# The shift of the weight decode as an integer product on GpSimd, and values scaled by two products

## The chip, the cores and the metric

The kernel runs on one core of a Trainium2 chip. The metric is the device time of one execution in microseconds. In the words of the profile, PE is TensorE's matmuls and PEld its weight loads, DVE is VectorE, ACT is ScalarE, POOL is GpSimd and SP is the engine that issues most DMAs.

## The reference

Attention with normalised queries and keys, and a feed-forward layer behind it. Inputs q and k are single precision, the four weight matrices come in double precision (the kernel sees each as pairs of 32-bit words).

```python
q_n, k_n = rmsnorm(q, g_q), rmsnorm(k, g_k)          # (8, 12, 448, 64)
attn = softmax(q_n @ k_n.T / sqrt(64)); attn_out = attn @ v
x = attn_out as (8 * 448, 768)
h = max(x @ w1, x @ w2, x @ w3)                      # each 768 x 768
out = h @ w_out                                      # (3584, 768)
```

## The kernel before

**The work.** There are 8 batches of 12 heads. Two heads of one batch are a group (48 groups). A group's keys and queries are squared, their squares summed, and rows scaled by the inverse root (a power, L387); the scores of a group are made in four parts of 112 rows for both heads. Each part goes from TensorE (L545 or L553) to VectorE's row maximum (L562), to ScalarE's exponentials (L570, L579), and after a transposition to TensorE again, which multiplies with the values (L692 or L703). The first six groups (`PLAIN`) use single precision in all matmuls. From group 6 on every operand is split into two half-precision parts: ScalarE makes the upper part, GpSimd or VectorE the lower (L440 for keys and queries, L531 for values, L665 for attention weights), and values are first scaled on GpSimd by a factor of the batch (`scale_v`, L517). When six groups of a batch are done, its feed-forward layer enters a queue from which TensorE gets some matmuls in each beat (L732, L796).

**The order.** It is written out by hand: the program runs rounds of twelve beats, one round a group, and each engine executes its instructions strictly in the order in which the beats issue them. `later(n, work, True)` puts work at the end of the beat n beats ahead. In round g (beats 0 to 11), GpSimd gets the squares of group g + 2 at beats 0 (keys) and 3 (queries); VectorE sums them at beats 2 and 5 (L372); GpSimd makes the inverse roots at beats 5 and 7 (L383, L387) and scales keys at beat 8 (L419, L423) and queries at beat 9 (L394, and L406 for groups from 6 on). VectorE makes row maxima at beats 2, 5, 8 and 11.

**The weight blocks.** The weights come as 24 blocks of 128 x 768 doubles: 18 of w1, w2, w3, then 6 of w_out. The doubles become floats by integer steps. ScalarE multiplies the upper words, read as floats, by a power of two (`rebias`, L188), which moves their exponent. Then `decode` makes the bits of the float in three stages, one beat after another: stage 0 (L196) shifts the upper word left by three, stage 1 (L200) puts back its sign bit, stage 2 (L205) puts in three bits of the lower word. All three are on VectorE before. Stages 1 and 2 read two tiles, the raw words and the float. A block starts at beats 1, 5 and 9 of rounds 0 to 5, and every eight beats after that, until the sixth block of w_out in round 9. Its three stages are issued 2, 3 and 4 beats later, at the ends of those beats: stage 0 at beats 3, 7, 11, and stage 1 at beats 4, 8, and 0 of the next round. When three blocks are there, VectorE takes their largest value (L170, 2304 columns), and later ScalarE scales them and makes the upper part (L268, L269), and GpSimd the lower part (L272).

Of the kernel before, what the change touches and what calls it, by code (L numbers as in the profile page):

```python
# [10 lines left out]
U32 = mybir.dt.uint32  # L11
F16 = mybir.dt.float16
AF = mybir.ActivationFunctionType
ALU = mybir.AluOpType
AX = mybir.AxisListType.X

P = 128
# [22 lines left out]
def qknorm_attention_maxout_ffn_kernel(  # L40
# [35 lines left out]
    nc = tc.nc  # L76
    B, H, S, D = q.shape
    DM, DF = w1.shape
    DO = w_out.shape[1]
    NP = H // 2  # L80
# [12 lines left out]
    const = ctx.enter_context(tc.tile_pool(name="const", bufs=1))  # L93
# [40 lines left out]
    half_neg = const.tile([P, 15], F32, name="half_neg")  # L134
    nc.vector.memset(half_neg, -0.5)

    sums = [const.tile([P, 15], F32, name=f"ss{i}") for i in range(2)]
    for t in sums:
        nc.vector.memset(t, 1.0)
# [50 lines left out]
    def decode(raw, f, stage):  # L190

        bits = raw.rearrange("p (n t) -> p n t", t=2)
        upper, lower = bits[:, :, 1], bits[:, :, 0]
        f = f.bitcast(U32)
        if stage == 0:
            nc.vector.tensor_scalar(  # L196
                out=f, in0=upper, scalar1=3, scalar2=None, op0=ALU.logical_shift_left
            )
        elif stage == 1:
            nc.vector.scalar_tensor_tensor(  # L200
                out=f, in0=upper, scalar=0x80000000, in1=f,
                op0=ALU.bitwise_and, op1=ALU.bitwise_or,
            )
        else:
            nc.vector.scalar_tensor_tensor(  # L205
                out=f, in0=lower, scalar=29, in1=f,
                op0=ALU.logical_shift_right, op1=ALU.bitwise_or,
            )
# [25 lines left out]
    def prep_block(n):  # L234
        kind, ft, j = blocks[n]
        raw = raws[n]
        f = plain(w_sb, n) if kind == "in" else plain(wo_sb, ft)
        rebias(raw)

        for stage in range(3):  # L240
            later(2 + stage, lambda stage=stage: decode(raw, f, stage), True)
        if kind == "out":
            later(5, lambda: row_largest(o_row[:, ft:ft + 1], f), True)
        later(5, load_raw)
        if j == NJ - 1:
            later(5, lambda: bound_in(ft), True)
        elif kind == "out" and ft == NFT - 1:
            later(6, bound_out)
# [234 lines left out]
    v_up = const.tile([P, B], F32, name="v_up")  # L483
# [31 lines left out]
    def scale_v(g):  # L515
        vr = st[g]["vr"]
        nc.gpsimd.tensor_scalar(  # L517
            out=vr, in0=vr, scalar1=v_up[:, g // NP:g // NP + 1], scalar2=None,
            op0=ALU.mult,
        )  # L520

    def upper_v(g):
# [338 lines left out]
    for i, src in enumerate((g_q, g_k)):  # L861
        nc.scalar.dma_start(
            out=gains[:, i], in_=src.rearrange("(o d) -> o d", o=1).broadcast_to([P, D])
# [61 lines left out]
    def beat(g, i):  # L925
# [80 lines left out]
        if PLAIN <= g < G and i == 9:  # L1006
            scale_v(g)
# [61 lines left out]
```

## Time and profile before

| what | value |
|---|---|
| runs, us | 1098.79, 1097.26, 1098.78; median 1098.78 |
| span of the profiled execution, us | 1101.6 |
| granted TensorE clock, mean | 0.957 |
| busy, us: PE / DVE / ACT / POOL | 1018.6 / 757.8 / 772.1 / 702.4 |
| the 24 shifts (L196) on VectorE, us | 11.8 (18 of w1 to w3) and 6.7 (6 of w_out) |
| the 42 value scalings (L517) on GpSimd, us | 60.7 |

The profiled execution has no device time of its own beside its span, which lies 2.8 us above the median of the runs. A row of a group says how many instructions it has, their busy time and mean, and how long the engine sat idle just before them and for whom. A row in order of time begins with its start and its length in microseconds. In the rows of stretches each engine has its busy time and the number of its instructions. Rounds can be told apart by the rows of `finish` (L718), one a round at its tenth or eleventh beat: in rounds 2 to 6 they start at 77.93, 99.83, 120.56, 142.66 and 168.33 us.

### The profile page before, as it was taken

What the parts mean: (1) busy time and instruction counts of PE and PEld (TensorE: products, weight loads), DVE (VectorE), ACT (ScalarE), POOL (GpSimd) and SP (SyncE); (2) the same over time, 40 slices, a digit from 0 to 9 for tenths busy, and PEclk for the clock granted to TensorE, in tenths of its full rate; (3) what the DMA queues carried; (4) which work ended last, traced back from release to release, by engine and by line L of the source; (5) the groups of instructions that cost most, each with busy time, mean ns of one, the idle gap of its engine ahead of it and who ended that gap; (6) DMA issues with size and microseconds to landing.
All of it is one profiled execution on the core that took longest, in us unless ns stands there. A gap on an engine that the chain in (4) does not pass through costs nothing. (4 is left out here: it accounts for less than half of the span.)

```text
span 1101.6 us, 18390 instructions
## 1 busy us (share of the span) xinstructions
PE 1018.6 (92%) x6168; PEld 501.9 (46%) x6168; DVE 757.8 (69%) x1390; ACT 772.1 (70%) x1767; POOL 702.4 (64%) x805
## 2 busy tenths in 40 slices
PE   4678768988999999999999999999999999999998
PEld 2334333434444455444544454444444454445555
DVE  3899988888667676677677776777677766762210
ACT  4599887767868678687877777778777787773001
POOL 5477988856767767678677686776867677610000
PEclk9687868998989999999999999999999999999999
DMA  5554466856787679877888789787877798563002
GB/s 149 165 164 152 129 180 137 179 115 125 151 166 149 134 151 172 160 148 133 176 155 149 136 169 175 141 151 150 170 146 143 145 166 153 106 106 73 1 1 58
DMA packets 426654, 152.29 MB, mean 138 GB/s; under 512 B 372928, under 2 KB 422336, under 8 KB 426560
## 3 DMA queue, kind: packets, MB, share of 16 engines
q1 hardware_dynamic: 425888, 150.75, 66.8%
q8 instruction: 48, 0.79, 0.3%
q10 hardware_dynamic: 672, 0.38, 0.1%
q14 instruction: 46, 0.38, 0.1%
HBM read 51.97 MB, written 11.01 MB: 57 GB/s over the span
## 5 line engine op out<-in xcount | busy, mean ns | idle before, releaser
L732 PE MATMUL acc<-xt,w_sb 128*128 128x448 f16 x2592 | 520.6, 356 | 0.6 <-ACT m L742 0.6
L732 PEld LDWEIGHTS <-w_sb 128*128 128x128 f16 x2592 | 245.1, 99 | 262.9 <-issue 53.1
L562 DVE TENSOR_REDUCE sc<-sc 112x2 f32<-112x896 f32 x192 | 209.7, 1092 | 47.8 <-PE sc L553 46.6
L579 ACT ACTIVATE sc<-sc,nm,down 112x448 f32<-112x448 f32 x336 | 234.2, 697 | 11.2
L655 ACT ACTIVATE pp<-sc,rs 112x448 f16<-112x448 f32 x336 | 194.8, 632 | 48.5 <-ACT sc L579 40.4
L665 DVE SCALAR_TENSOR_TENSOR pp<-sc,rs,pp 112x448 f16<-112x448 f32 x336 | 212.9, 675 | 3.4 <-ACT pp L655 2.9
L387 POOL TENSOR_TENSOR ri<-ri,half_neg 128x7 f32<-128x7 f32 x96 | 154.2, 1606 | 8.0
L553 PE MATMUL sc<-kt,qt 64*112 64x448 f16 x1008 | 133.7, 371 | 27.1 <-DVE pp L665 23.6
L570 ACT ACTIVATE nm<-sc,down 112x2 f32<-112x2 f32 x192 | 50.7, 264 | 149.5 <-DVE sc L562 148.2
L796 PE MATMUL acc<-wo_sb,ht 128*128 128x384 f16 x864 | 151.4, 330 | 1.4 <-DVE ht L756 0.8
L761 POOL COPY hx<-ht 128x128 f16<-128x128 f16 x48 | 15.5, 323 | 197.7 <-DVE ht L756 191.7
L796 PEld LDWEIGHTS <-ht 128*128 128x128 f16 x864 | 82.0, 99 | 67.5 <-issue 14.5
L703 PE MATMUL av<-pt,vp 128*64 128x448 f16 x1008 | 108.3, 356 | 0.0
L553 PEld LDWEIGHTS <-qt 64*112 64x112 f16 x1008 | 55.0, 128 | 96.9 <-issue 56.4
L648 DVE TENSOR_SCALAR rs<-sc 112x2 f32<-112x2 f32 x168 | 26.6, 158 | 94.7 <-ACT sc L579 94.7
L440 POOL TENSOR_TENSOR kp<-kn,kp 128x512 f16<-128x512 f32 x42 | 50.0, 1190 | 58.9 <-ACT kp L434 58.9
L703 PEld LDWEIGHTS <-vp 128*64 128x64 f16 x1008 | 49.6, 108 | 56.0 <-issue 30.4
L718 DVE SCALAR_TENSOR_TENSOR xt<-av,xt 128x448 f16<-128x448 f32 x42 | 26.2, 625 | 71.1 <-ACT xt L717 71.1
L372 DVE TENSOR_REDUCE ss<-sq 128x7 f32<-128x448 f32 x96 | 60.9, 635 | 10.6 <-ACT sq L363 6.6
L531 POOL TENSOR_TENSOR vp<-vr,vp 128x448 f16<-128x448 f32 x42 | 43.8, 1044 | 32.2 <-ACT vp L525 32.1
L440 POOL TENSOR_TENSOR qp<-qn,qp 112x512 f16<-112x512 f32 x42 | 49.3, 1173 | 21.0 <-ACT qp L434 20.8
L517 POOL TENSOR_SCALAR vr<-vr,v_up 128x448 f32<-128x448 f32 x42 | 60.7, 1446 | 0.0
(112 smaller groups left out, 1203.1 us busy)
## 6 DMA issues: line engine op xcount, KB each, us to landing
raw<-in_moe_w_dram SPq DMA_DIRECT2D x18, 768.0 KB, 4.4
qr<-in_q_dram SPq DMA_DIRECT2D x48, 224.0 KB, 3.0
vr<-in_v_dram SPq DMA_DIRECT2D x96, 96.0 KB, 2.5
kr<-in_k_dram SPq DMA_DIRECT2D x95, 96.0 KB, 3.0
raw<-in_moe_w_out_dram SPq DMA_DIRECT2D x6, 768.0 KB, 5.1
pt<-pp SPq DMA_TRANSPOSE x168, 4.1
out_dram<-osb SPq DMA_DIRECT2D x8, 336.0 KB, 3.2
out_dram<-osb SPq DMA_DIRECT2D x8, 288.0 KB, 3.7
```

Of the source, the lines that this page charges most:

```text
L372: nc.vector.tensor_reduce(sums[g % 2][:sq.shape[0], KQ[what]], sq, axis=AX, op=ALU.add)
L387: nc.gpsimd.tensor_tensor(out=ri, in0=ri, in1=half_neg[:, at], op=ALU.pow)
L440: nc.gpsimd.tensor_tensor(out=parts[:, 1], in0=n, in1=parts[:, 0], op=ALU.subtract)
L517: nc.gpsimd.tensor_scalar(out=vr, in0=vr, scalar1=v_up[:, g // NP:g // NP + 1], scalar2=None, op0=ALU.mult,)
L553: nc.tensor.matmul(sc[:QP, h, :S], qt[rows, qp, c], kt[rows, kp, KEYS[h]], start=n == 0, stop=n == len(TERMS) - 1,)
L562: nc.vector.tensor_reduce(sc[:QP, 0, S + 8:S + 10], sc[:QP, :, :S], axis=AX, op=ALU.max, negate=True)
L579: nc.scalar.activation(to, sc[:QP, h, :S], AF.Exp, bias=nm[:, h:h + 1], scale=down[:QP], accum_out=total,)
L655: nc.scalar.activation(pp[:, 0, h], sc[:QP, h, :S], AF.Copy, scale=rs[:, h:h + 1])
L665: nc.vector.scalar_tensor_tensor(out=pp[:, 1, h], in0=sc[:QP, h, :S], scalar=rs[:, h:h + 1], in1=pp[:, 0, h], op0=ALU.mult, op1=ALU.subtract,)
L703: nc.tensor.matmul(av[half, :S], vp[rows, group, vpart], pt[rows, 7 * wp + group], start=u == 0 and n == 0, stop=u == 3 and n == len(TERMS ...
L732: nc.tensor.matmul(acc[:, :S], wt[:, wp, c], xs[c][:, xp], start=(c == 0 and n == 0), stop=(c == NCT - 1 and n == 2),)
L796: nc.tensor.matmul(acc[:, :HW], lhs, wo_sb[:, f, wp, half * HW:(half + 1) * HW], start=(f == 0 and n == 0), stop=(f == NFT - 1 and n == 2),)
```

## The change

Stage 0 is issued on GpSimd: the upper word times eight, both unsigned integers, where the eight is one column that is broadcast over the 768. Its place in the program, the end of its beat, is the same. A constant column is set once at the start. The value scaling on GpSimd gets a second product with 1.0 in the same instruction.

```diff
+    eight = const.tile([P, 1], U32, name="eight")
+    nc.vector.memset(eight, 8)
...
         if stage == 0:
-            nc.vector.tensor_scalar(
-                out=f, in0=upper, scalar1=3, scalar2=None, op0=ALU.logical_shift_left
+            nc.gpsimd.tensor_tensor(
+                out=f, in0=upper, in1=eight.broadcast_to([P, DM]), op=ALU.mult
             )
...
         nc.gpsimd.tensor_scalar(
-            out=vr, in0=vr, scalar1=v_up[:, g // NP:g // NP + 1], scalar2=None,
-            op0=ALU.mult,
+            out=vr, in0=vr, scalar1=v_up[:, g // NP:g // NP + 1], scalar2=1.0,
+            op0=ALU.mult, op1=ALU.mult,
         )
```

Every line of the kernel behind the constant stands three lines further down after the change (L196 becomes L199, L200 becomes L203, L372 becomes L375).

GpSimd's rows from the second inverse root (beat 7) of round 4 to the squares at beat 0 of round 5, before. `ri` are the inverse roots, `kn` the scaled keys, `qn` the queries, `w_sb` the weights; the number behind a name tells two buffers apart:

```order
L383 TENSOR_SCALAR ri<-ss_86 128x8
L387 TENSOR_TENSOR ri<-ri,half_neg 128x8
L419 TENSOR_TENSOR kn_90<-kr,ri 128x3x64
L423 TENSOR_TENSOR kn_90<-kr,ri 64x64
L419 TENSOR_TENSOR kn_90<-kr,ri 128x3x64
L423 TENSOR_TENSOR kn_90<-kr,ri 64x64
L272 TENSOR_TENSOR w_sb<-w_sb 128x768
L394 TENSOR_TENSOR qn<-qr,ri 112x2x4x64
L406 TENSOR_TENSOR qn<-qn,gain 112x512
L365 TENSOR_TENSOR sq<-kr 128x448
```

The same stretch of GpSimd after the change:

```order
L386 TENSOR_SCALAR ri<-ss_88 128x8
L390 TENSOR_TENSOR ri<-ri,half_neg 128x8
L199 TENSOR_TENSOR w_sb<-raw,eight 128x768
L422 TENSOR_TENSOR kn_92<-kr,ri 128x3x64
L426 TENSOR_TENSOR kn_92<-kr,ri 64x64
L422 TENSOR_TENSOR kn_92<-kr,ri 128x3x64
L426 TENSOR_TENSOR kn_92<-kr,ri 64x64
L275 TENSOR_TENSOR w_sb<-w_sb 128x768
L397 TENSOR_TENSOR qn<-qr,ri 112x2x4x64
L409 TENSOR_TENSOR qn<-qn,gain 112x512
L199 TENSOR_TENSOR w_sb<-raw,eight 128x768
L368 TENSOR_TENSOR sq<-kr 128x448
```

Two products (L199) have come into it: one between the inverse root and the keys, one between the queries and the next squares. The third product of a round stands behind the squares of the queries at beat 3.

VectorE's rows from the end of `finish` in round 3 to the row maximum at beat 2 of round 4, before (`xt` is the attention's result, `sc` the scores, `w_most` and `w_up` the scale of three blocks):

```order
L718 SCALAR_TENSOR_TENSOR xt<-av,v_up,xt 128x448
L562 TENSOR_REDUCE sc<-sc 112x2
L196 TENSOR_SCALAR w_sb<-raw 128x768
L259 TENSOR_SCALAR w_most<-most 128x1
L262 RECIPROCAL w_up<-w_most 128x1
L263 TENSOR_SCALAR w_up<-w_up 128x1
L200 SCALAR_TENSOR_TENSOR w_sb<-raw,w_sb 128x768
L205 SCALAR_TENSOR_TENSOR w_sb<-raw,w_sb 128x768
L562 TENSOR_REDUCE sc<-sc 112x2
```

The same stretch of VectorE after:

```order
L721 SCALAR_TENSOR_TENSOR xt<-av,v_up,xt 128x448
L565 TENSOR_REDUCE sc<-sc 112x2
L262 TENSOR_SCALAR w_most<-most 128x1
L265 RECIPROCAL w_up<-w_most 128x1
L266 TENSOR_SCALAR w_up<-w_up 128x1
L203 SCALAR_TENSOR_TENSOR w_sb<-raw,w_sb 128x768
L208 SCALAR_TENSOR_TENSOR w_sb<-raw,w_sb 128x768
L565 TENSOR_REDUCE sc<-sc 112x2
```

The shift is gone from it, and L203 reads what GpSimd's product wrote.

## The prediction

> **What bounds the kernel now.** I read the page first, then the busy time by stretches, then the groups of instructions of the two engines that the change touches, and last their rows in order of time in the rounds that mattered.
>
> ```profile
> span 1101.6 us, 18390 instructions
> core 0: us, PE busy (x) PEld busy (x) DVE busy (x) ACT busy (x) POOL busy (x), PEclk, DMA share, GB/s
> 20.00:60.00 40.00, 27.43 (x139) 14.93 (x140) 30.63 (x42) 24.92 (x61) 21.42 (x26) 0.74 0.48 143
> 80.00:150.00 70.00, 52.47 (x269) 26.96 (x269) 65.21 (x81) 63.08 (x138) 61.37 (x49) 0.74 0.50 147
> 150.00:245.00 95.00, 80.53 (x446) 36.48 (x442) 83.07 (x139) 69.72 (x150) 73.30 (x72) 0.89 0.72 153
> 245.00:1000.00 755.00, 739.36 (x4655) 359.94 (x4656) 540.37 (x1062) 574.46 (x1340) 522.24 (x622) 0.99 0.77 148
> ```
>
> From 245 us on TensorE is busy 739.36 of 755 us: it is the bound, and whatever is late or early by then is carried to the end undiminished. All weight blocks are decoded before that. In 80 to 150 us the bound is VectorE, 65.21 of 70 us, with GpSimd close behind at 61.37; in 150 to 245 us nothing is full. So the change is decided in the first 245 us. That VectorE is waited for there shows in the chain of waits of 10 to 245 us, where ScalarE's softmax stands behind VectorE's row maximum, and TensorE's scores behind that softmax (total, times, longest):
>
> ```profile
> ACT nm L570 <- DVE sc L562: 27.4, 12, 5.0
> PE sc L545 <- ACT e L579: 14.8, 12, 4.0
> ```
>
> The shift that goes, the step after it, and the nearest relative of the product that comes (minimum/median/maximum ns); then the shift's sums, for 80 to 150 us and for w_out's blocks; last the value scaling:
>
> ```profile
> L196 DVE TENSOR_SCALAR w_sb<-raw x18: 537/550/1326, 23.2 to 144.3; 128x768 uint32<-128x768 uint32 x18
> L205 DVE SCALAR_TENSOR_TENSOR w_sb<-raw,w_sb x18: 936/954/4292, 29.4 to 148.3; 128x768 uint32<-128x768 uint32 x18
> L272 POOL TENSOR_TENSOR w_sb<-w_sb x18: 1630/1640/1907, 66.8 to 200.2; 128x768 f16<-128x768 f32 x18
> L196 DVE TENSOR_SCALAR w_sb<-raw 128x768 uint32<-128x768 uint32 x10 | 5.9, 591 | 0.0
> L196 DVE TENSOR_SCALAR wo_sb<-raw 128x768 uint32<-128x768 uint32 x6 | 6.7, 1110 | 0.1
> L517 POOL TENSOR_SCALAR vr<-vr,v_up x42: 1400/1410/2230, 169.1 to 982.2; 128x448 f32<-128x448 f32 x42
> ```
>
> L205 has a median of 954 ns and a maximum of 4292. That worst one, with GpSimd's rows beside it:
>
> ```profile
> 123.80 1.65 POOL L365 TENSOR_TENSOR sq<-kr 128x448 f32<-128x448 f32 x1
> 124.69 4.29 DVE L205 SCALAR_TENSOR_TENSOR w_sb<-raw,w_sb 128x768 uint32<-128x768 uint32 x1
> 125.41 1.64 POOL L272 TENSOR_TENSOR w_sb<-w_sb 128x768 f16<-128x768 f32 x1
> 127.00 1.16 POOL L440 TENSOR_TENSOR kp<-kn,kp 128x512 f16<-128x512 f32 x1
> 128.12 1.87 POOL L440 TENSOR_TENSOR qp<-qn,qp 112x512 f16<-112x512 f32 x1
> ```
>
> It ended at 128.98; 0.95 us before that is 128.03, just before GpSimd went from one row to the next. So VectorE's steps with two inputs stand still while GpSimd works on large tiles, and GpSimd's do the same in turn: the same shape at L440 took 1.16 without VectorE, and the next, smaller one 1.87. The Trainium skill (SBUF — State Buffer, "Who interferes with whom") says that a VectorE instruction with two SBUF inputs contends with a GpSimd instruction that reads SBUF, under a lock that the first one holds whole. The rows of this case agree for large tiles.
>
> **The change, term by term.** I write M for one product on GpSimd. No row shows an integer product. The floor is the same width as a subtraction, 1.64 us (L272); the other end is the slowest elementwise rate of the rows, L517, 1.41 x 768 / 448 = 2.42 us. I take the middle, 2.0 us, since integers are further from both. Below nothing is excluded: it is an added instruction on its engine.
>
> *VectorE's side*: 24 shifts go. At 0.55 us undisturbed that is 13.2 us; a shift, too, was at times blocked (1.11 us on average for w_out).
>
> *The rounds before 78 us* (9 blocks): 9 x 0.55 = 5.0 us of VectorE at most. But in 20 to 60 us VectorE is idle for 9.4 of 40 us, on loads, ScalarE and TensorE, and GpSimd for 18.6, so M finds room and the shift had room too. One thing costs: in the first round M of the third block stands ahead of the next squares on GpSimd and waits for ScalarE's rebias of it.
>
> ```profile
> 33.55 0.93 POOL L365 TENSOR_TENSOR sq<-kr 128x448 f32<-128x448 f32 x1
> 40.72 0.88 ACT L188 ACTIVATE raw<-raw 128x768 f32<-128x768 f32 x1 [2.96 <-DMA raw<-in_moe_w_dram]
> ```
>
> The squares that ran at 33.55 now start after 41.6 + M = 43.6. I take -0.5, ends -5 and +3.
>
> *Rounds 3, 4 and 5 (78 to 143 us)*, the term that decides. In each round two of the three M stand where GpSimd's work after the second sum of squares (L372) leads to VectorE's first decode step of the next round (L200): one ahead of the keys, one after the queries. Before, these ends of GpSimd's stretch held up nobody. Now L200 must wait for them. Each round's L200, its reduction L372 of q, the shift between them, and the end of GpSimd's stretch:
>
> ```profile
> 80.45 1.34 DVE L200 SCALAR_TENSOR_TENSOR w_sb<-raw,w_sb 128x768 uint32<-128x768 uint32 x1
> 88.98 0.55 DVE L196 TENSOR_SCALAR w_sb<-raw 128x768 uint32<-128x768 uint32 x1
> 91.44 0.68 DVE L372 TENSOR_REDUCE ss<-sq 112x8 f32<-112x512 f32 x1
> 98.98 1.76 POOL L394 TENSOR_TENSOR qn<-qr,ri 112x512 f32<-112x512 f32 x1
> 102.35 1.23 DVE L200 SCALAR_TENSOR_TENSOR w_sb<-raw,w_sb 128x768 uint32<-128x768 uint32 x1
> 109.88 0.99 DVE L196 TENSOR_SCALAR w_sb<-raw 128x768 uint32<-128x768 uint32 x1
> 112.78 0.68 DVE L372 TENSOR_REDUCE ss<-sq 112x8 f32<-112x512 f32 x1
> 122.22 1.61 POOL L406 TENSOR_TENSOR qn<-qn,gain 112x512 f32<-112x512 f32 x1
> 123.08 1.57 DVE L200 SCALAR_TENSOR_TENSOR w_sb<-raw,w_sb 128x768 uint32<-128x768 uint32 x1
> 132.96 0.55 DVE L196 TENSOR_SCALAR w_sb<-raw 128x768 uint32<-128x768 uint32 x1
> 135.41 0.68 DVE L372 TENSOR_REDUCE ss<-sq 112x8 f32<-112x512 f32 x1
> 145.79 1.85 POOL L406 TENSOR_TENSOR qn<-qn,gain 112x512 f32<-112x512 f32 x1
> 145.18 1.35 DVE L200 SCALAR_TENSOR_TENSOR w_sb<-raw,w_sb 128x768 uint32<-128x768 uint32 x1
> ```
>
> Round 3: from L200 to the end of L372, 92.12 - 80.45 = 11.67, less its shift 0.55; from there to the end of GpSimd's stretch, 100.74 - 92.12 = 8.62; with 2 M = 4.0 the way round is 23.74 us, against 102.35 - 80.45 = 21.90 now: +1.8. Round 4: 11.11 - 0.99 + 10.37 + 4.0 = 24.49 against 20.73: +3.8. Round 5: 13.01 - 0.55 + 11.55 + 4.0 = 28.01 against 22.10: +5.9. Together +11.5. That counts twice what the two engines make each other wait: while VectorE stands still behind M it blocks nobody, and a single L205 here holds 3.3 us of such waiting (4.29 - 0.95). I take 1.5 us a round off, 4.5 in all: **+7**. M counts six times in it: with 1.64 it is +4.8, with 2.42 +9.5. Behind L200 in VectorE's queue stand L205 and then the row maximum L562, for which ScalarE and TensorE wait as above, so this is paid in full. The third M of a round, ahead of the conversion of the weights at L272, has the room in which GpSimd now waits and costs nothing; without that room it would cost up to M each, 6 us.
>
> *Rounds 6 to 9 (143 to 245 us)*: six blocks, one every eight beats. Six shifts worth 6.7 us go from VectorE, which is behind here: TensorE waits for it before its scores.
>
> ```profile
> PE sc L553 <- DVE pp L665: 13.0, 7, 3.9
> ```
>
> GpSimd is busy 73.3 of 95 us and takes 6 M = 12 more, without a loop as above since only one M lies on the way and the rounds are longer. But keys and queries come up to M later. I take -2; ends -6.7 and +6.
>
> *Values (L517)*: 42 instructions, none before 169.1 us. A second product could make one as short as the squares of this width, 0.93 us (L365 at 33.55), or add the part that goes by elements again, up to twice 1.41. Where TensorE is busy 98% of the time this costs and gains nothing; its cover would have to be worn through by 42 x 1.41 = 59 us on GpSimd, which has 755 - 522 = 233 us idle there. Only four or so lie before 245 us: 0, ends -2 and +6. The memset of the constant (one column, once) is nothing.
>
> Sum: -0.5 + 7 - 2 + 0 = **+4.5 us**. The profiled execution has a span of 1101.6 us, 2.8 above the median of the runs, 1098.78; I take the profile's difference onto the median: 1103.3 us. About 0.2%, 2.2 us, is what a measurement of this kernel can tell from no change.
>
> **The rivals.** *Relief of VectorE*: VectorE is the fullest engine in 80 to 150 us and loses 10 shifts, 5.9 us, and half of w_out's 6.7; GpSimd, no longer blocked by shifts, has M done before L200 asks. For it: the shift's maximum of 1326 ns and w_out's mean of 1110 show that shift and GpSimd blocked each other. Against it: the three rounds above, where GpSimd's end lay at most 1.6 us before L200 (100.74 against 102.35) and after it in the other two. It decides where two M fit into what the mutual waiting gives back: M under about 0.8 us by my term for these rounds (7 - 6 x 1.2 = 0). Part of the 9.3 us will be lost to other engines; I price it at -7: 1091.8 us.
>
> *A slow integer product*: the power at L387 shows that an operation can cost GpSimd far more than a product of floats. At M = 3.2 the three rounds get 6 x 1.2 = 7 more, the two rounds before them close the same way (+2 each), and four later rounds lose about 1 each: 4.5 + 7 + 4 + 4, about +19: 1118 us. It would begin to show at M over 2.4.
>
> *The lock for every instruction*: if any GpSimd instruction held VectorE off for its whole length, pushing the power (1.5 us) onto VectorE's L200 and L205 would cost one such wait more in each of rounds 3 to 5, 3 x 1.5 = 4.5 us: 1107.8. Against it:
>
> ```profile
> 156.81 1.48 POOL L387 TENSOR_TENSOR ri<-ri,half_neg 128x7 f32<-128x7 f32 x1
> 157.45 0.94 DVE L200 SCALAR_TENSOR_TENSOR wo_sb<-raw,wo_sb 128x768 uint32<-128x768 uint32 x1
> ```
>
> L200 ran at its undisturbed length inside a power. The Trainium skill (SBUF — State Buffer, "SBUF: two separate sides") states the lock for the whole instruction; by that the time would be this one, and these two rows speak against it for a tile of 7 columns.
>
> *Nothing to measure*: the mutual waiting gives back 3 us a round, not 1.5, and the terms cancel: 1098.8.
>
> **How the numbers follow.** Forecast, VectorE waiting for GpSimd in rounds 3 to 5: 0.43, of which 0.33 lies above 0.2% and 0.10 within. Relief: 0.28. Slow product: 0.12. Lock for all: 0.05. Nothing: 0.12. So faster 0.28, same 0.22, slower 0.50. The forecast's own range, with M from 1.64 to 2.42 and the early and late terms' inner halves, is 1098 to 1109. The range for 8 in 10 reaches down past the centre of the relief, to 1090.5, and up to 1115, most of the way to the slow product.
>
> **What would show it.** In the profile after: the product's rows at 1.6 to 2.4 us; L200 (now L203) of the first beat of rounds 4 to 6 with VectorE idle before it, released by GpSimd's product, 1 to 3 us each; rounds of 23 to 25 us where they were 21.9, 20.7 and 22.1; GpSimd over 90% busy in 80 to 150 us; TensorE's share after 245 us unchanged. Wrong it would be if VectorE's idle time before L203 is small and the rounds get shorter, or if the product is far from 2.0 us. The value scaling should change its own rows and nothing else.

## The result and the profile after

The changed kernel took 1113.99 us (median of 4 runs, 1113.11 to 1114.81), the kernel before 1098.26 beside it (4 runs, 1097.26 to 1098.79): a ratio of 1.0141, interval 1.0127 to 1.0156, or +15.7 us where +4.5 was predicted. The direction was right, the size was not.

First the head of the page and the busy time by stretches after. The rounds are longer, so the last stretch begins at 257 instead of 245 us.

```profile
span 1112.9 us, 18428 instructions
80.00:150.00 70.00, 49.27 (x233) 24.13 (x232) 58.42 (x56) 50.67 (x109) 53.98 (x48) 0.74 0.43 125
257.00:1012.00 755.00, 738.36 (x4662) 359.48 (x4661) 540.98 (x1063) 574.16 (x1341) 491.38 (x622) 1.00 0.77 148
```

TensorE is busy 738.36 of 755 us in the long last stretch, as before (739.36), so the loss came earlier and was carried. In 80 to 150 us no engine is full now: VectorE fell from 65.21 to 58.42 and GpSimd from 61.37 to 53.98. That is less work done in 70 us, by engines that wait; GpSimd was predicted at over 90%, and is at 77%.

Where the time went is read from the starts of the rounds' `finish`. One thing has to be known for it: in every run with both figures the device time is 1.7 to 2.1 us above the span, so the profiled execution of before, with a span of 1101.6, lies some 5 us above the median. For the rounds I therefore compare with an experiment whose decode is that of before (values_only, below; span 1096.7, time 1098.51). Rounds 2 to 6 of that kernel, then of the kernel after:

```profile
76.55 0.68 DVE L718 SCALAR_TENSOR_TENSOR xt<-av,v_up,xt 128x448 f16<-128x448 f32 x1 [1.19 <-ACT xt L717]
98.43 0.68 DVE L718 SCALAR_TENSOR_TENSOR xt<-av,v_up,xt 128x448 f16<-128x448 f32 x1
119.60 0.69 DVE L718 SCALAR_TENSOR_TENSOR xt<-av,v_up,xt 128x448 f16<-128x448 f32 x1 [1.83 <-ACT xt L717]
142.28 0.68 DVE L718 SCALAR_TENSOR_TENSOR xt<-av,v_up,xt 128x448 f16<-128x448 f32 x1 [1.33 <-ACT xt L717]
168.07 0.69 DVE L718 SCALAR_TENSOR_TENSOR xt<-av,v_up,xt 128x448 f16<-128x448 f32 x1 [0.19 <-ACT xt L717]
```

```profile
78.34 0.67 DVE L721 SCALAR_TENSOR_TENSOR xt<-av,v_up,xt 128x448 f16<-128x448 f32 x1
104.28 0.67 DVE L721 SCALAR_TENSOR_TENSOR xt<-av,v_up,xt 128x448 f16<-128x448 f32 x1
130.23 0.67 DVE L721 SCALAR_TENSOR_TENSOR xt<-av,v_up,xt 128x448 f16<-128x448 f32 x1
156.44 0.67 DVE L721 SCALAR_TENSOR_TENSOR xt<-av,v_up,xt 128x448 f16<-128x448 f32 x1
184.69 0.69 DVE L721 SCALAR_TENSOR_TENSOR xt<-av,v_up,xt 128x448 f16<-128x448 f32 x1 [0.19 <-ACT xt L720]
```

The lag of the kernel after is 1.8 us at round 2, 5.9 at round 3, 10.6, 14.2 at round 5 and 16.6 at round 6; by round 11 it is 15.7 (302.03 against 286.32), and the spans differ by 16.2 (1112.9 against 1096.7). So rounds 3, 4 and 5, which end at the second to fourth row, cost 14.2 - 1.8 = +12.4 us: 25.94, 25.95 and 26.21 long. The early rounds cost +1.8, and all behind 156 us +1.5 to +2. These small terms are no surer than a single trace: in the profile of before, round 2's row starts at 77.93, which would leave +0.4 for the early rounds and +13.4 for rounds 3 to 5.

The product and the value scaling (minimum/median/maximum ns), by tile and by line after:

```profile
L199 POOL TENSOR_TENSOR w_sb<-raw,eight x18: 1463/1470/2180, 22.0 to 160.7; 128x768 uint32<-128x768 uint32 x18
L520 POOL TENSOR_SCALAR vr<-vr,v_up x42: 632/637/646, 185.4 to 993.5; 128x448 f32<-128x448 f32 x42
```

M is 1.47 us, less than my floor of 1.64. The product was cheap, and yet the loss was over three times the forecast. What grew are VectorE's two steps behind it. Their groups before, 20 to 262 us (busy time and mean ns, idle time just before them):

```profile
L205 DVE SCALAR_TENSOR_TENSOR w_sb<-raw,w_sb 128x768 uint32<-128x768 uint32 x18 | 27.7, 1538 | 0.2
L200 DVE SCALAR_TENSOR_TENSOR w_sb<-raw,w_sb 128x768 uint32<-128x768 uint32 x18 | 20.2, 1120 | 0.2
```

The same after:

```profile
L203 DVE SCALAR_TENSOR_TENSOR w_sb<-raw,w_sb 128x768 uint32<-128x768 uint32 x18 | 37.3, 2074 | 22.0 <-POOL w_sb L199 22.0
L208 DVE SCALAR_TENSOR_TENSOR w_sb<-raw,w_sb 128x768 uint32<-128x768 uint32 x18 | 22.3, 1237 | 0.2
```

L203 waits 22.0 us for the product; at beat 0 such a wait was predicted. But it also got 17.1 us longer itself, 37.3 against 20.2, which was not predicted. L208 got 5.4 us shorter than L205, so the two steps together take 59.6 us against 47.9. In order of time, GpSimd's rows and VectorE's two steps at beat 0 of round 3, and the steps at beat 0 of rounds 4 and 5:

```profile
81.26 1.47 POOL L199 TENSOR_TENSOR w_sb<-raw,eight 128x768 uint32<-128x768 uint32 x1
82.69 0.93 POOL L368 TENSOR_TENSOR sq<-kr 128x448 f32<-128x448 f32 x1
82.76 7.29 DVE L203 SCALAR_TENSOR_TENSOR w_sb<-raw,w_sb 128x768 uint32<-128x768 uint32 x1 [2.29 <-POOL w_sb L199]
83.58 1.65 POOL L275 TENSOR_TENSOR w_sb<-w_sb 128x768 f16<-128x768 f32 x1
85.19 1.04 POOL L368 TENSOR_TENSOR sq<-qr 112x512 f32<-112x512 f32 x1
86.18 1.46 POOL L199 TENSOR_TENSOR w_sb<-raw,eight 128x768 uint32<-128x768 uint32 x1
87.61 1.63 POOL L275 TENSOR_TENSOR w_sb<-w_sb 128x768 f16<-128x768 f32 x1
90.09 0.97 DVE L208 SCALAR_TENSOR_TENSOR w_sb<-raw,w_sb 128x768 uint32<-128x768 uint32 x1
...
108.70 7.31 DVE L203 SCALAR_TENSOR_TENSOR w_sb<-raw,w_sb 128x768 uint32<-128x768 uint32 x1 [2.30 <-POOL w_sb L199]
...
135.99 3.28 DVE L203 SCALAR_TENSOR_TENSOR w_sb<-raw,w_sb 128x768 uint32<-128x768 uint32 x1 [3.63 <-POOL w_sb L199]
139.30 3.91 DVE L208 SCALAR_TENSOR_TENSOR w_sb<-raw,w_sb 128x768 uint32<-128x768 uint32 x1
```

L203 starts 0.07 us after the squares and ends at 90.05, 0.81 us behind GpSimd's last tile (87.61 + 1.63 = 89.24). L208, undisturbed, takes 0.97. So it got no turn for five tiles in a row, 6.5 us, while every one of GpSimd's tiles ran at its undisturbed length (squares 0.93, not 1.64). In round 4 the same happened; in round 5 L203 got its turn after two tiles and L208 stood still instead. The same place before:

```profile
80.94 1.64 POOL L365 TENSOR_TENSOR sq<-kr 128x448 f32<-128x448 f32 x1
81.83 3.17 DVE L205 SCALAR_TENSOR_TENSOR w_sb<-raw,w_sb 128x768 uint32<-128x768 uint32 x1
82.55 1.64 POOL L272 TENSOR_TENSOR w_sb<-w_sb 128x768 f16<-128x768 f32 x1
84.15 1.75 POOL L365 TENSOR_TENSOR sq<-qr 112x512 f32<-112x512 f32 x1
86.88 1.64 POOL L272 TENSOR_TENSOR w_sb<-w_sb 128x768 f16<-128x768 f32 x1 [0.98 <-ACT w_sb L269]
```

Here L205 stood behind the rest of the squares and all of L272. It lost the boundary between them at 82.55 and got its turn at about 84.1, where L272 ended, and the next squares took 1.75 instead of 1.04: VectorE won that boundary. Behind these squares GpSimd paused for 0.98 us, for ScalarE. After the change a product stands in the place of the pause.

The Trainium skill (SBUF — State Buffer, "SBUF: two separate sides") says that whichever of the two engines starts first holds the shared access for its whole instruction, and the other blocks. By that, if the blocked engine came next, L203 would lose the rest of one tile, under 0.9 us. This trace shows more: five instructions, one behind the other, held it off for 6.5.

Behind L203 and L208 stands the row maximum, for which ScalarE's softmax waits. The row of the chain that cost 27.4 us in 12 waits before, now in 10 to 257 us:

```profile
ACT nm L573 <- DVE sc L565: 40.8, 18, 5.1
```

### The profile page after: what moved, and what is told of

Same layout as the page of the kernel before. It is cut to its first block, busy times and chain, and to the rows that moved or that the text cites. A ratio compares the mean times of both kernels' runs of the same rounds, so it can differ in the third digit from the quotient of the medians.

```text
span 1112.9 us, 18428 instructions
## 1 busy us (share of the span) xinstructions
PE 1020.9 (92%) x6168; PEld 502.4 (45%) x6168; DVE 751.1 (67%) x1367; ACT 771.8 (69%) x1767; POOL 692.6 (62%) x829
## 5 line engine op out<-in xcount | busy, mean ns | idle before, releaser
L735 PEld LDWEIGHTS <-w_sb 128*128 128x128 f16 x2592 | 244.4, 98 | 259.4 <-issue 48.3
L556 PE MATMUL sc<-kt,qt 64*112 64x448 f16 x1008 | 131.9, 367 | 27.8 <-DVE pp L668 23.5
L390 POOL TENSOR_TENSOR ri<-ri,half_neg 128x7 f32<-128x7 f32 x96 | 150.2, 1565 | 8.0
L375 DVE TENSOR_REDUCE ss<-sq 128x7 f32<-128x448 f32 x96 | 60.8, 634 | 10.6 <-ACT sq L366 6.6
L755 ACT ACTIVATE ht<-acc 128x448 f16<-128x448 f32 x48 | 26.3, 548 | 41.7 <-DVE acc L749 41.7
```

The costliest lines, as they stand in the source:

```text
L375: nc.vector.tensor_reduce(sums[g % 2][:sq.shape[0], KQ[what]], sq, axis=AX, op=ALU.add)
L390: nc.gpsimd.tensor_tensor(out=ri, in0=ri, in1=half_neg[:, at], op=ALU.pow)
L556: nc.tensor.matmul(sc[:QP, h, :S], qt[rows, qp, c], kt[rows, kp, KEYS[h]], start=n == 0, stop=n == len(TERMS) - 1,)
L735: nc.tensor.matmul(acc[:, :S], wt[:, wp, c], xs[c][:, xp], start=(c == 0 and n == 0), stop=(c == NCT - 1 and n == 2),)
```

## Experiments

Diffs are against the changed kernel where nothing else is said. A ratio is to the kernel before, run beside it.

### The two halves of the change: values_only and shift_only

The first keeps VectorE's shift, the second the scaling with one product.

```diff
# values_only
-            nc.gpsimd.tensor_tensor(
-                out=f, in0=upper, in1=eight.broadcast_to([P, DM]), op=ALU.mult
+            nc.vector.tensor_scalar(
+                out=f, in0=upper, scalar1=3, scalar2=None, op0=ALU.logical_shift_left
# shift_only
-            out=vr, in0=vr, scalar1=v_up[:, g // NP:g // NP + 1], scalar2=1.0,
-            op0=ALU.mult, op1=ALU.mult,
+            out=vr, in0=vr, scalar1=v_up[:, g // NP:g // NP + 1], scalar2=None,
+            op0=ALU.mult,
```

> The value scaling with two products alone, the shift stays on VectorE. If the loss is all in the decode: L517 at 0.64 us as in the changed kernel, and the time that of before within 0.2% (0 to -1.5 us), since no GpSimd row of that kind is waited for. If the shorter value scaling upsets the order of transfers or of GpSimd's rows in rounds 6 to 9: slower by 2 us or more.

> The product of integers on GpSimd alone, values scaled with one product. If the loss is all in the decode: slower than before by 14 to 17 us, as the whole change. If the value scaling gave back part of a larger loss in rounds 6 to 9: slower by 18 us or more.

values_only: 1097.68 us, ratio 0.9997 (0.9988 to 1.0007). shift_only: 1115.74, 1.0163 (1.0147 to 1.0179). On the kernel before, the values change nothing although their 42 instructions fell from 1.41 to 0.64 us at the median; the loss is the decode's. Beside the changed decode they may save a little (1115.74 against 1113.99), but the two intervals overlap.

### Where in the program: room

The nine blocks of rounds 3 to 5 keep VectorE's shift, the fifteen others have the product.

```diff
+            if 9 <= n < 18:
+                nc.vector.tensor_scalar(
+                    out=f, in0=upper, scalar1=3, scalar2=None, op0=ALU.logical_shift_left
+                )
+            else:
+                nc.gpsimd.tensor_tensor(
```

> The whole change, but the nine blocks that are decoded in rounds 3 to 5 keep VectorE's shift; the other fifteen are products on GpSimd. Theory, starvation: the loss comes from rounds 3 to 5 alone, where GpSimd has five large tiles in a row behind the product and VectorE's L203 gets no turn for 7.3 us; the rounds go back to 21 to 22 us and the time is that of before or 1 to 4 us less. Rival, load: each product costs a share of the 15.7 us (0.65 us each); fifteen of them give +9 to +10 us.

1099.16 us, ratio 1.0017 (1.0008 to 1.0027). Nearly all of the loss goes with these nine blocks. The fifteen other products cost 0.9 to 3 us by the interval; they gain nothing.

### Is it the wait or the shared access: ghost

VectorE keeps its shifts and waits for no product; GpSimd makes 23 products at the same places into tiles that nobody reads.

```diff
+            if n < 23:
+                spare = plain(w_sb, min(n + 2, 17)) if n < 17 else plain(wo_sb, n - 17)
+                nc.gpsimd.tensor_tensor(
+                    out=spare.bitcast(U32), in0=upper,
+                    in1=eight.broadcast_to([P, DM]), op=ALU.mult,
+                )
+            nc.vector.tensor_scalar(
+                out=f, in0=upper, scalar1=3, scalar2=None, op0=ALU.logical_shift_left
```

> VectorE keeps all shifts and waits for no product; GpSimd makes the products all the same, at the same places of its order, into buffers that are not read before they are written anew (23 of 24; values with two products). It is the change's load on GpSimd and on what the two engines share, without the wait. Theory, the shared access: VectorE's two-input steps meet rows of large tiles on GpSimd as in the changed kernel, one of them takes 4 to 7 us in rounds 3 to 5, and the time is 1102 to 1108 us (the values alone give 1097.7). Rival, the wait for the product is what matters: GpSimd's extra work holds up nobody: 1097 to 1100 us.

1118.90 us, ratio 1.0179 (1.0163 to 1.0196): above the ranges of both expectations, and as much as the change or more, without a single wait of VectorE for a product. Its two steps (L209 and L214 here) at beat 0 of round 3, in order of time:

```profile
82.73 1.95 DVE L209 SCALAR_TENSOR_TENSOR w_sb<-raw,w_sb 128x768 uint32<-128x768 uint32 x1
84.71 6.61 DVE L214 SCALAR_TENSOR_TENSOR w_sb<-raw,w_sb 128x768 uint32<-128x768 uint32 x1
```

And their sums over 20 to 262 us:

```profile
L214 DVE SCALAR_TENSOR_TENSOR w_sb<-raw,w_sb 128x768 uint32<-128x768 uint32 x18 | 37.5, 2082 | 0.2
L209 DVE SCALAR_TENSOR_TENSOR w_sb<-raw,w_sb 128x768 uint32<-128x768 uint32 x18 | 24.5, 1362 | 0.2
```

Together 62.0 us against 47.9 before: 14.1 us more of standing still, with no idle time ahead of them. That the product comes late is therefore not needed for a loss of this size; that GpSimd runs it there is enough. But ghost is not the change without its wait. VectorE has its shifts on top of GpSimd's products, and GpSimd is so late that ScalarE's upper part of the weights (L278) waits for the lower part of the block before (L281), 8.6 us in five waits from 20 to 262 us. Neither the kernel before nor the changed one has such waits. How the 19.6 us are divided between VectorE's steps and ScalarE's waits is not shown.

### Which product of a round: m3_vector, m7_vector, m11_vector

In every round 0 to 5 one of the three products goes back to VectorE's shift: the one of beat 3, 7 or 11. The diff is that of m3_vector; the other two have 1 and 2 where it has the first 0.

```diff
-            nc.gpsimd.tensor_tensor(
+            if n % 3 == 0 and n < 18:
+                nc.vector.tensor_scalar(
+                    out=f, in0=upper, scalar1=3, scalar2=None, op0=ALU.logical_shift_left
+                )
+            else:
+                nc.gpsimd.tensor_tensor(
```

> The whole change, but the six blocks of w1 to w3 whose stage 0 is issued at beat 3 keep VectorE's shift. Theory, no pause: this product closes the gap in which GpSimd waited for ScalarE before its second L275, and VectorE's L203 got its turn in that gap; with the gap back L203 at beat 0 falls from 7.3 to 3.3 us and the time by 6 to 10 us, far over one third of the loss: 1104 to 1108 us. Rival, the way round by the products at beats 7 and 11: this product lies beside it, and nothing changes: 1112 to 1115 us.

> The whole change, but the six blocks of w1 to w3 whose stage 0 is issued at beat 7 (ahead of the keys) keep VectorE's shift. By the way round, each such product is on it: 1.5 us a product and 0.9 us less contention in rounds 3 to 5, 1106 to 1110 us. By the missing pause: the five large tiles behind beat 11 stay together, L203 at beat 0 still takes 7 us, 1110 to 1114 us.

> The whole change, but the six blocks of w1 to w3 whose stage 0 is issued at beat 11 (ahead of the squares of the next round) keep VectorE's shift. VectorE then reaches L203 at beat 0 without waiting and ahead of GpSimd's row of large tiles. By both theories most of the loss goes: 1098 to 1104 us. If load alone counts, one third of it at most: 1109 us or more.

m3_vector: 1110.05 us, 1.0106 (1.0091 to 1.0121). m7_vector: 1110.85, 1.0116 (1.0094 to 1.0137). m11_vector: 1097.47, 0.9994 (0.9984 to 1.0005). Without the product of beat 11 nothing is lost; this takes away VectorE's wait at beat 0 and part of the row at once, so it does not tell the two apart. Without that of beat 3 or 7 some 3 to 4 us less are lost; m3_vector lies between the ranges of its two expectations. The three gains, 3.9, 3.1 and 16.5 us, add up to more than the loss of 15.7, so the products don't act one by one. In m3_vector, the first step (L208) and the squares of the queries:

```profile
84.15 3.27 DVE L208 SCALAR_TENSOR_TENSOR w_sb<-raw,w_sb 128x768 uint32<-128x768 uint32 x1 [2.30 <-POOL w_sb L204]
86.57 1.75 POOL L373 TENSOR_TENSOR sq<-qr 112x512 f32<-112x512 f32 x1
```

With one product less, VectorE wins the boundary ahead of these squares (3.27 instead of 7.29, and they are slowed to 1.75), with the same wait for the product of beat 11 ahead of it, 2.30 us. So the product of beat 3, which the prediction took for free, costs 4 us.

m7_vector came out within the range of the missing pause, but not by its mechanism: L203 (L208 there) at beat 0 was to stay at 7 us and took 3.27 to 3.28 in rounds 3 to 5. In round 4 the same five tiles follow each other without a pause, at the same distances as in the changed kernel, and VectorE won the boundary ahead of the squares of the queries. Its second step then took 4.71 us (3.12 in round 3), so the two steps together stood there nearly as long: 7.98 us against 8.27. So the same row can hold off either step, with about the same sum.

### A pause made on purpose: give_way and give_both

GpSimd gets a copy of one column that needs VectorE's step of beat 0 (give_way: the first of the two steps, give_both: the second), so it must stop there.

```diff
+            if n < 18 and n % 3 == 2:
+                nc.gpsimd.tensor_copy(turn_stile, f[:, :1])
```

> The whole change and one more instruction on GpSimd in six blocks: a copy of one column of the float, issued behind the L203 that comes at beat 0, so that GpSimd must wait until this L203 is done. The output is not touched. Theory, starvation: L203 at beat 0 of rounds 4 and 5 falls from 7.3 to 3.4 us or less (the squares of the keys and one L275 ahead of it, 0.93 + 1.64, then 0.95), and the time falls by 5 to 8 us against the changed kernel, although a wait and an instruction are added. Rival, lateness of the product: what costs is that VectorE waits for the product and GpSimd has more to do; the added wait makes it slower by 0 to 5 us.

> As the run that gives way once, but the copy of one column stands behind the last decode stage (L208) of the same six blocks, so that GpSimd stays off until both of VectorE's steps are done; the output is not touched. Theory, moved starvation: giving way once only moved the long wait from L203 (7.3 to 3.3 us) to L208 (1.0 to 4.8 us), since VectorE gets its turns only where GpSimd stops. With both: L203 3.3 us, L208 1.0 us, about 4 us less in each of rounds 3 and 4 and some in 5: 1103 to 1107 us. Rival, GpSimd's load: it stops for two steps more and is late for keys and queries; 1113 to 1118 us.

The expectations count the rounds of the 7.3 us steps as 4 and 5; by the rows of `finish` they are 3 and 4. give_way: 1116.95 us, 1.0174 (1.0160 to 1.0188), a miss of the theory; the time is the one that the rival gave, 3.0 us slower. In order of time:

```profile
84.88 3.27 DVE L204 SCALAR_TENSOR_TENSOR w_sb<-raw,w_sb 128x768 uint32<-128x768 uint32 x1 [1.66 <-POOL w_sb L200]
85.68 1.66 POOL L278 TENSOR_TENSOR w_sb<-w_sb 128x768 f16<-128x768 f32 x1
88.22 0.19 POOL L209 COPY turn_stile<-w_sb 128x1 uint32<-128x1 uint32 x1 [0.88 <-DVE w_sb L204]
88.44 4.80 DVE L211 SCALAR_TENSOR_TENSOR w_sb<-raw,w_sb 128x768 uint32<-128x768 uint32 x1 [0.29 <-POOL turn_stile L209]
```

GpSimd paused and the first step got its turn (3.27), as the theory had it. Then GpSimd's next tiles held off the second (4.80): the wait moved on by one instruction. With the pause behind the second step, give_both:

```profile
103.70 3.27 DVE L204 SCALAR_TENSOR_TENSOR w_sb<-raw,w_sb 128x768 uint32<-128x768 uint32 x1 [2.30 <-POOL w_sb L200]
107.01 0.96 DVE L209 SCALAR_TENSOR_TENSOR w_sb<-raw,w_sb 128x768 uint32<-128x768 uint32 x1
```

1105.15 us, 1.0065 (1.0049 to 1.0081): a pause long enough for both steps brings back 8.8 of 15.7 us, with every product still on GpSimd and the wait of 2.30 us still there. Rounds 3 and 4 are 21.83 and 22.11 us long instead of 25.94 and 25.95. What is left I put down to that wait and to what GpSimd loses by pausing; no run separates the two.

### Small instructions between the large tiles: gaps_all, gaps_shift, gaps_m11

Behind every square, product and lower part of rounds 2 to 5 GpSimd copies one column, and waits for nobody in it. gaps_all has the whole change, gaps_shift has VectorE's shifts, gaps_m11 those of beat 11.

```diff
+    def gap():
+        if 24 <= clock[0] < 76:
+            nc.gpsimd.tensor_copy(gap_out, gap_in)
```

> The whole change, and in rounds 2 to 5 a copy of one column on GpSimd, which waits for nobody, behind every square, weight difference (L275) and product: about eight a round of 0.2 us. Theory, a small instruction is break enough: VectorE's two-input steps begin while GpSimd runs the small copy; L203 at beat 0 of rounds 4 and 5 falls from 7.3 to 2 us or less, and 5 to 12 us of the loss go: 1101 to 1108 us. Rival, only standing still helps: as long as GpSimd has work, VectorE gets its turn by chance; L203 stays at 7 us and the copies make it slower, 1114 to 1120 us.

> The same small copies behind squares and weight differences in rounds 2 to 5, with all shifts on VectorE and values by two products (1097.7 without them). If a small instruction is break enough: the L205 of 2.2 to 4.3 us at beat 1 fall to 2 or less, 1092 to 1096 us, faster than both kernels. If not: 1097 to 1101 us.

> The same small copies on the version whose products at beat 11 are VectorE's shifts again (1097.5 without them). If a small instruction is break enough: 1090 to 1095 us. If not: 1097 to 1102 us.

gaps_all: 1107.83 us, 1.0084 (1.0071 to 1.0098). gaps_shift: 1099.67, 1.0010 (1.0001 to 1.0018). gaps_m11: 1098.19, 0.9994 (0.9985 to 1.0003). In gaps_all, in order of time (L211 and L216 are VectorE's steps, L142 the copy):

```profile
83.09 0.18 POOL L142 COPY gap_out<-gap_in 128x1 f32<-128x1 f32 x1
83.18 0.96 DVE L211 SCALAR_TENSOR_TENSOR w_sb<-raw,w_sb 128x768 uint32<-128x768 uint32 x1 [2.42 <-POOL w_sb L206]
83.23 1.70 POOL L377 TENSOR_TENSOR sq<-kr 128x448 f32<-128x448 f32 x1
84.17 3.30 DVE L216 SCALAR_TENSOR_TENSOR w_sb<-raw,w_sb 128x768 uint32<-128x768 uint32 x1
84.88 0.18 POOL L142 COPY gap_out<-gap_in 128x1 f32<-128x1 f32 x1
85.02 1.64 POOL L283 TENSOR_TENSOR w_sb<-w_sb 128x768 f16<-128x768 f32 x1
86.61 0.91 POOL L142 COPY gap_out<-gap_in 128x1 f32<-128x1 f32 x1
```

L211 came in during a copy and took its undisturbed 0.96 us instead of 7.29; the squares paid, 1.70. L216 got no turn at the copy at 84.88; it ended at 87.47, so it ran during that of 86.61, which was itself held up and took 0.91. So a small instruction can be break enough for VectorE to get its turn, but not each time. This brings back about 6 of 15.7 us. In gaps_shift and gaps_m11 the copies didn't shorten the long steps: at beat 1 of rounds 3 to 5 these took 3.29, 2.41 and 4.54 us in gaps_shift, where values_only has 3.17, 2.28 and 4.29, and the time stayed as well. What a shorter step would be worth there, these two runs can't say.

### The lower parts out of the way: spaced_all, spaced_m11, spaced_shift, spaced_part

The lower part (L275) of a block is made two beats later, and the copy of give_both is kept. spaced_all has the whole change, spaced_m11 has VectorE's shift at beat 11, spaced_shift everywhere; spaced_part is spaced_shift for the first 12 blocks' lower parts alone, with the copy behind five blocks instead of six.

```diff
-                later(4 + 4 * j, lambda n=n, f=f: lower(n, f), True)
+                later(6 + 4 * j, lambda n=n, f=f: lower(n, f), True)
```

> The whole change, the copy of one column behind the last decode stage of six blocks as in the run that gives way for both, and the lower parts of the weights (L275) two beats later, so that at beats 0 and 1 only the squares of the keys stand between the product and GpSimd's stop. The output is not touched. By starvation: L203 at beat 0 takes 1.9 us at most and L208 1.0; 1.6 us less than the run that gives way for both in each of rounds 3 to 5: 1099 to 1103 us. What is then left over the values alone (1097.7) is the price of waiting for the product. By GpSimd's load: no better than 1105 us.

> The same two edits on the version whose products at beat 11 are VectorE's shifts again (1097.5). By starvation, VectorE's second two-input step at beat 1, 2.3 to 4.4 us there, falls to 1.0: 1091 to 1095 us, faster than both kernels. If GpSimd's stop costs as much as VectorE gains: 1096 to 1100 us.

> The same two edits with every shift on VectorE, that is, the kernel before with values by two products (1097.7). By starvation the long L205 at beat 1 (2.3 to 4.3 us in rounds 3 to 5) falls to 1.0: 1091 to 1095 us. If VectorE's long steps were covered by other waits in those rounds: 1096 to 1099 us.

> All shifts on VectorE, values by two products, the lower parts of the first twelve blocks two beats later and GpSimd's stop behind L205 for five blocks; the last six blocks' lower parts where they were. The version with all of them moved gained 2.6 us by round 5 on the values alone and lost it in rounds 6 and 7, where the lower parts pushed queries back. If that is the cause: 1094 to 1096 us. If the loss in rounds 6 and 7 has another cause: 1097 to 1100 us.

spaced_all: 1109.77 us, 1.0092 (1.0078 to 1.0107). spaced_m11: 1104.90, 1.0054 (1.0040 to 1.0069). spaced_shift: 1098.51, 0.9997 (0.9988 to 1.0005). spaced_part: 1097.82, 0.9996 (0.9987 to 1.0004). All missed the gain hoped for. At beat 0 the two steps took 1.67 and 0.96 us in spaced_all, as expected, but L278, now between the inverse roots, was itself held up (2.65 instead of 1.64), and rounds 6 and 7 took 27.8 and 29.9 us, against 28.3 and 26.9 in the changed kernel and 25.8 and 26.0 in values_only. spaced_part was 2.9 us ahead of values_only at the end of round 5, having begun 0.5 ahead, and lost most of it in round 6 (27.4 against 25.8), though the last six lower parts were back in their places; why is open. spaced_shift is a warning: over 20 to 262 us VectorE's two steps took 41.2 us instead of 48.3 (values_only), and the time did not change. spaced_all says the same: its two steps at beat 0 are 1.6 us a round shorter than give_both's, but rounds 3 to 5 together take 69.98 us against 69.61. So a step that stands still is not paid for at its full length wherever it stands. No version beats the kernel before by more than its measurement can tell.

## Why the prediction was wrong in size

**The place: right.** The loss lies in rounds 3 to 5 (+12.4 of 15.7), and room shows that it goes with their products. VectorE is idle for the product ahead of L203 at beat 0, for 2.30, 3.63 and 3.63 us in rounds 4 to 6, within or just above the forecast 1 to 3. Rounds came out at 26 us, longer than the forecast 23 to 25.

**The step that failed: VectorE's stretch, taken over from before, and "I take 1.5 us a round off".** The sum of the way round gave +11.5 with M = 2.0, or 11.5 - 6 x 0.53 = +8.3 with the measured 1.47. From it the prediction subtracted 4.5, since VectorE and GpSimd would make each other wait less. The same way after runs from L203 at beat 0 (82.76, 108.70, 135.99) over the end of L375 of the queries to the next L203 at beat 0:

```profile
96.90 0.67 DVE L375 TENSOR_REDUCE ss<-sq 112x8 f32<-112x512 f32 x1
122.84 0.67 DVE L375 TENSOR_REDUCE ss<-sq 112x8 f32<-112x512 f32 x1
149.05 0.67 DVE L375 TENSOR_REDUCE ss<-sq 112x8 f32<-112x512 f32 x1
162.20 3.27 DVE L203 SCALAR_TENSOR_TENSOR w_sb<-raw,w_sb 128x768 uint32<-128x768 uint32 x1 [3.63 <-POOL w_sb L199]
```

The three ways take 79.44 us in all, where they took 64.73 in the profile of before: +14.7 (more than the +12.4 above, since the base is another trace and the last way ends in round 6). GpSimd's stretch, from the end of L375 to the next L203 without the two products, takes 8.19, 9.54 and 9.54 us, where the prediction's rows had 8.62, 10.37 and 11.55: 3.3 us less, so the relief came on GpSimd's side. VectorE's stretch, from L203 to the end of L375, takes 14.81, 14.81 and 13.73 us, where the prediction had 11.12, 10.12 and 12.46 with the shift taken off: 9.7 us more. That is the two steps at beat 0: L203 and L208 took 8.3, 8.3 and 7.2 us, 23.7 in all, where L200 and L205 had taken 4.5, 3.5 and 5.9, 13.9 in all. So the way round lies 6.4 above the raw sum, not 4.5 below it. The argument "while VectorE stands still behind M it blocks nobody" is true and shows in GpSimd's undisturbed rows; what it left out is that VectorE, once the product is there, meets GpSimd's row of large tiles. The sign stood in the prediction's own rows: the L205 of 4.29 us let GpSimd go from one tile to the next at 125.41 and at 127.00 before it got its turn at 128.03.

**The mechanism under it.** The forecast was a wait of VectorE for the product. That wait is there, but ghost has none of it and loses 19.6 us. There VectorE's steps with two inputs get no turn beside GpSimd's row of large tiles, and ScalarE waits for GpSimd besides. In the changed kernel the first of these is shown by give_both and gaps_all, which leave products and wait in place and give VectorE a turn: 8.8 and about 6 us come back. For the other 7 us of the loss I take the wait as the main cause, since the way round counts +8.3 by the products alone; no run shows it by itself.

**"The third M costs nothing": wrong.** It has the room in which GpSimd waited, but that room was also VectorE's: m3_vector, without this product, is 3.9 us faster. The prediction named 6 us as the price if the room were not there, and gave it no chance.

**M: too high.** 1.47, below both ends. The rival of the slow product is refuted, though its time, 1118, lay nearer to the result than the forecast; how near a time comes says nothing for its mechanism.

**Early and late rounds: small, and no gain.** +0.4 to +1.8 against -0.5, and +1.5 to +2 against -2. room bears out that together they gain nothing.

**Values: right,** 0, at 0.64 us each, shorter than either end given.

**The other rivals.** Relief of VectorE is refuted: the shifts of 0.55 us that it was spared were repaid by steps that stood still for up to 7.3. *Nothing to measure* fails with the forecast, since it took still more off for mutual waiting. The lock for every instruction isn't needed for the loss, and these runs don't settle it: a copy of one column was held up by VectorE itself (0.91 instead of 0.18 us), but it is too short to show whether it would hold VectorE off.

**What stays open.** Which engine gets the turn at the boundary of two GpSimd tiles. VectorE won the one ahead of the squares of the queries before, in m3_vector and in m7_vector, and lost the same one in rounds 3 and 4 of the changed kernel, with the same tiles on both sides. Why the loss is so uneven over the three products may follow from that rule, and is not settled.

## What to carry to other kernels

Where two engines share an access, don't ask whether the second engine has free time for one more large tile, but whether the first one still gets its turn between the tiles: a pause of GpSimd, here 1.9 us in give_both, let both of VectorE's two-input steps through, while between two tiles without a pause they got their turn only at times. A queue on the path that stands beside an unbroken row can lose several times what the moved instruction costs; look for rows whose length in the trace is several times their minimum, and see what ended them. A pause put in for one instruction passes the wait to the next, so it has to cover all that must come through.

## What the runs showed of the hardware

A two-input VectorE step of 0.95 us took 7.29 and 7.31 us behind five GpSimd tiles in a row, not behind one; with the same five tiles in m7_vector it took 3.27 and the next one 4.71. A GpSimd copy of one column, 0.18 us, can be a break in which such a step starts at full speed (0.96 us), and the copy takes 0.91 us when VectorE has come first. An unsigned product over 128 x 768 with a broadcast column takes 1.47 us on GpSimd, less than the subtraction of floats into half precision of that size (1.63 to 1.65). And a second product with 1.0 made a scaling of 448 columns shorter, 0.637 against 1.41 us; why was not looked into.
